# Seven half-size second products for two chunks of the first block, with their sums and the attention steps around them placed anew

## The chip, the cores and the metric

The kernel runs on one core of a Trainium2 chip. The core has five engines with queues of their own: TensorE (PE in the profile; its weight loads are listed apart as PEld), VectorE (DVE), ScalarE (ACT), GpSimd (POOL) and SyncE (SP), which issues most DMAs. Each engine takes its instructions in the order in which the program issues them and waits on semaphores for the others. The metric is the device time of one execution in microseconds (us).

## The reference

The program computes a linear attention with decay over 4 batches, 8 heads, 768 tokens and head size 64, and then a feed-forward layer with a squared relu:

```python
state = gamma * state + k[:, :, t] (outer) v[:, :, t]     # for each token t, per batch and head
y[:, :, t] = scale * q[:, :, t] @ state                   # scale = 1 / sqrt(64)
x = y, as 3072 tokens x 512
h = maximum(x @ w_in, 0)                                  # w_in  512 x 2048
out = (h * h) @ w_out                                     # w_out 2048 x 512
```

Inputs and output are float32 in HBM.

## The kernel before

**Tiling.** The 3072 tokens are 24 chunks of 128 (six for each batch). The feed-forward layer takes them in 11 blocks (`BLOCKS`, line 19): four chunks in block 0 and two in each other block. The hidden size 2048 is 16 groups f of 128; four groups are a quarter g. Matmuls read bf16 and accumulate in float32 in PSUM, in banks that hold 512 float32 values per partition.

**A block's feed-forward** (`ffn_pieces`, line 976) is a generator that yields after each piece of TensorE work. The first product (line 826) makes x @ w_in for a group f; ScalarE takes the relu out of PSUM into an `h` tile (line 835), and the squares are taken a little later by VectorE (line 806) or ScalarE. The second product multiplies the squares with w_out:

- In blocks 0 and 1 it is plain (`second`, line 1019): 16 matmuls of 512 columns for a chunk, one per f, into one bank. In block 0 all four chunks go together, quarter by quarter: g outside, chunks inside, so four banks are open. `store` (line 1030) has ScalarE copy each bank to `osb` and SyncE issue the output's DMA.
- From block 2 on (`SEVEN`) the two chunks are handled by `seven_products` (line 840). It is Strassen's scheme in Winograd's form: the two chunks, the two halves of the 2048 hidden values (even and odd f) and the two halves of the 512 outputs make a 2 x 2 by 2 x 2 product of blocks, done with seven half-size products of eight 256-wide matmuls each, where the plain way has eight. VectorE makes sums of the h blocks (`s1` to `s4`) and adds the products (`u`, `v`, `oa`, `ob`). The sums of w_out's blocks (`t1` to `t4`, tiles `w_sum`) are made once by `sum_w_out` (line 313): half 0 is made from w_out's quarters 0 and 1, half 1 from quarters 2 and 3. The seventh product of a block is kept (`kept`) and run among the first products of the next block.

**The loads of w_out.** Four DMAs on GpSimd's queue (`load_w_out`, line 169) bring a quarter each and convert it to bf16. They are issued at places 6, 8, 11 and 14.

**The order** is written out by hand. All engines' queues follow the program's order. `n` counts pieces: block 0's first four come before the loop, its first products for f = 4 to 15 are pieces 5 to 16, its second products pieces 17 to 32, and block 1 begins with piece 33. After piece n, `before(n)` (line 1204) issues what `put(n, ...)` has registered: the attention steps of later chunks, loads, casts and sums of w_out; and then the squares that are due. I say "place n" for that. `attend(m, scaled, places)` registers the steps of one chunk m: `scale_q` and `transpose_q` (for an even m, for both chunks of a pair: VectorE; then TensorE and a ScalarE copy), `scale_kv` (k on VectorE, v on GpSimd), `transpose_k` (TensorE, two ScalarE copies to `k_bd`), `scores` in two halves (TensorE, then VectorE's mask), `state` (TensorE, then ScalarE copies one half of the rows and VectorE the other) and `outputs` (TensorE, a ScalarE copy to `xt`).

**Buffers that matter here.** The pool `ps_f` (tiles `psf`) has four banks; `tp`, `st`, `y` and `c_ps` have one each, and transposes of q and of k share `tp`. `hpool` has three tiles of 4096 columns: `spare` (line 1052), which holds masked scores at the start, and the two h tiles of block 0; later blocks take one each in turn. `opool` has four output tiles. The tile framework makes an engine wait before it touches a PSUM bank of a tile that another engine still uses.

Of the kernel before, what the change touches and what calls it, by code (L numbers as in the profile page):

```python
# [9 lines left out]
FP32 = mybir.dt.float32  # L10
# [3 lines left out]
AF = mybir.ActivationFunctionType  # L14
ALU = mybir.AluOpType
# [16 lines left out]
def kernel(  # L32
# [9 lines left out]
    nc = tc.nc  # L42
    P = nc.NUM_PARTITIONS

    B, H, S, D = q.shape
    DM, DFF = moe_w_in.shape
    C = 128
    NCH = S // C
    NPAIR = H // 2
    NFB = DFF // 128  # L50
    NCB = DM // 128
    NQ = 4
    FPQ = NFB // NQ
# [22 lines left out]
    opool = ctx.enter_context(tc.tile_pool(name="opool", bufs=4))  # L76
    upool = ctx.enter_context(tc.tile_pool(name="upool", bufs=1))
# [4 lines left out]
    ps_f = ctx.enter_context(tc.tile_pool(name="ps_f", bufs=4, space=bass.MemoryType.PSUM))  # L82
# [105 lines left out]
    def exponents(pattern, step, name, logs, parts=(slice(0, P),)):  # L188
# [35 lines left out]
        out=ident[:],  # L224
# [11 lines left out]
        out=cmask[:],  # L236
# [10 lines left out]
    for rows in halves:  # L247
        nc.gpsimd.affine_select(
            out=maskp[rows],
# [58 lines left out]
    w_out_bf = [t[:, j * FPQ : (j + 1) * FPQ] for t in w_out_halves for j in range(2)]  # L308

    HN = DM // 2  # L310
    sums = [const.tile([P, NFB // 2, HN], BF16, name=f"w_sum{i}") for i in range(4)]

    def sum_w_out(half):

        src = w_out_halves[half].rearrange("s (j k) (n c) -> s k n j c", k=2, n=2)
        (b11, b12), (b21, b22) = ([src[:, k, n] for n in range(2)] for k in range(2))
        t1, t2, t3, t4 = (t[:, 4 * half : 4 * half + 4] for t in sums)
        for out, in0, in1 in ((t1, b12, b11), (t2, b22, t1), (t3, b22, b12), (t4, b21, t2)):
            yield nc.vector.tensor_tensor(out=out, in0=in0, in1=in1, op=ALU.subtract)
# [489 lines left out]
    h2s = {}  # L809

    def h_tiles(tb):
        wide = BLOCKS[tb] * C
        count = NFB * wide // 4096
        for _ in range(count):
            t = hpool.tile([P, 4096], BF16, name="h2")
            h2s.setdefault(tb, []).append(t.rearrange("e (f t) -> e f t", t=wide))

    def h_of(tb, f0, f1=None):
        n = NFB // len(h2s[tb])
        j, f = divmod(f0, n)  # L820
        return h2s[tb][j][:, f : f + (1 if f1 is None else f1 - f0)]

    def first_product(tb, hp, f, cols):
        g, fq = divmod(f, FPQ)
        for cb in range(NCB):
            nc.tensor.matmul(  # L826
                hp,
                lhsT=w_in_bf[g][:, cb, fq * 128 : (fq + 1) * 128],
                rhs=xts[tb][:, cb, cols],
                start=(cb == 0),  # L830
                stop=(cb == NCB - 1),
            )

    def relu(hv, hp, on_scalar=False):
        nc.scalar.activation(hv, hp[:], AF.Relu)  # L835
        squares.append((hv, on_scalar))

    kept = []

    def seven_products(tb):  # L840
# [115 lines left out]

        return first_sums, rest if tb + 1 < len(BLOCKS) else rest_at_end

    open_ps = {}

    def first_unit(tb, g, c, parts=(0, 1)):

        if tb not in h2s:
            h_tiles(tb)
        if (tb, g, c) not in open_ps:
            open_ps[tb, g, c] = ps_f.tile([P, FPQ, C], FP32, name="psf")
        hp = open_ps[tb, g, c]
        cols = slice(c * C, (c + 1) * C)
        half = FPQ // 2
        for part in parts:  # L970
            for fq in range(part * half, (part + 1) * half):
                first_product(tb, hp[:, fq, :], g * FPQ + fq, cols)
        if 1 in parts:
            relu(h_of(tb, g * FPQ, (g + 1) * FPQ)[:, :, cols], open_ps.pop((tb, g, c)))

    def ffn_pieces(tb):
        nch = BLOCKS[tb]
        TB = nch * C
        if tb == 0:
            for f in range(FPQ, NFB):  # L980
                hp = ps_f.tile([P, TB], FP32, name="psf")
                first_product(tb, hp[:], f, slice(0, TB))
                relu(h_of(tb, f)[:, 0], hp)
                yield
        elif tb <= 2:

            for c in range(nch):
                for g in range(NQ):
                    first_unit(tb, g, c)
                    if tb in SEVEN and (c, g) == (1, 3):  # L990
                        first_sums, rest = seven_products(tb)
                        first_sums(slice(0, 4))
                    yield
            if tb in SEVEN:
                yield from rest()
                return
        else:
            h_tiles(tb)
            per = 512 // TB
            if tb in SEVEN:  # L1000
                first_sums, rest = seven_products(tb)
            for f0 in range(0, NFB, per):
                hp = ps_f.tile([P, per, TB], FP32, name="psf")
                for f in range(f0, f0 + per):
                    first_product(tb, hp[:, f - f0, :], f, slice(0, TB))
                relu(h_of(tb, f0, f0 + per), hp, tb in SEVEN and f0 // per in (1, 3))
                if f0 // per in (1, 2, 3) and kept:
                    next(kept[0])
                if f0 // per == 4:
                    kept.clear()  # L1010
                if f0 // per == 5 and tb in SEVEN:
                    first_sums(slice(0, 4))
                yield
            if tb in SEVEN:
                yield from rest()
                return


        def second(op, j, g, cols=slice(0, DM)):
            for fq in range(FPQ):  # L1020
                f = g * FPQ + fq
                nc.tensor.matmul(  # L1022
                    op[:],
                    lhsT=h_of(tb, f)[:, 0, j * C : (j + 1) * C],
                    rhs=w_out_bf[g][:, fq, cols],
                    start=(f == 0),
                    stop=(f == NFB - 1),
                )

        def store(op, j, cols=slice(0, DM)):  # L1030
            osb = opool.tile([P, DM], FP32, name="osb")
            nc.scalar.activation(osb[:, cols], op[:], AF.Copy)
            r0 = (first[tb] + j) * C
            nc.sync.dma_start(out[r0 : r0 + C, cols], osb[:, cols])


        together = nch if tb == 0 else 1
        for j0 in range(0, nch, together):
            ops = [ps_f.tile([P, DM], FP32, name="psf") for _ in range(together)]
            for g in range(NQ):  # L1040
                for j, op in enumerate(ops):
                    second(op, j0 + j, g)
                    if g == NQ - 1:
                        store(op, j0 + j)
                    yield


    tp, st, f = (ps_tp, "tp"), (ps_st, "st"), (ps_f, "psf")
# [3 lines left out]
    spare = hpool.tile([P, 4096], BF16, name="h2")  # L1052
# [68 lines left out]
    start = [sum(npieces[:tb]) for tb in range(len(BLOCKS) + 1)]  # L1121
    parts = {}

    def put(place, what, *args):
        parts.setdefault(place, []).append((what, args))
# [4 lines left out]
    def attend(m, scaled, places):  # L1130
        if m % 2 == 0:
            put(scaled, scale_q, m, 0)
            put(scaled, scale_q, m, 1)
            put(places[0], transpose_q, m)
        put(places[0], scale_kv, m)
        put(places[1], transpose_k, m)
        put(places[2], scores, m, 0)
        put(places[3], scores, m, 1)
        put(places[3], state, m)
        put(places[4], outputs, m)  # L1140
# [20 lines left out]
    for m, which, place in ((6, "k", 16), (6, "v", 17), (7, "k", 18), (7, "v", 19)):  # L1161
        put(place, load_kv, m, which)
    put(10, cast_w, "in", 3)
    for half, at_places in enumerate(((25, 25, 25, 25), (31, 31, 48, 48))):
        made = sum_w_out(half)
        for place in at_places:
            put(place, next, made)
    attend(4, 21, (23, 25, 27, 29, 31))
    attend(5, None, (28, 30, 31, 32, 34))
    attend(6, 31, (33, 35, 37, 39, 42))  # L1170
    attend(7, None, (38, 42, 44, 46, 49))
    packed = pack_constants()
# [13 lines left out]
    for m, d in zip(range(PACK_FROM, NCHUNK), done):  # L1186
# [4 lines left out]
    places = {  # L1191
        (8, "k"): [22, 23, 24, 25, 33, 33, 34, 34],
        (8, "v"): [35 + j // 2 for j in range(8)],
        (12, "k"): [47, 48, 49, 50, 52, 53, 55, 56] + [74 + j for j in range(8)],
        (12, "v"): [58, 59, 60, 61, 62, 64, 65, 66] + [82 + j for j in range(8)],
        (18, "k"): [92 + 4 * j // 3 for j in range(8)] + [117 + 4 * j // 3 for j in range(8)],
        (18, "v"): [103 + 4 * j // 3 for j in range(8)] + [128 + 4 * j // 3 for j in range(8)],
    }
# [10 lines left out]
    n = BLOCKS[0]  # L1209
    before(n)  # L1210
    for tb in range(len(BLOCKS)):
        for _ in ffn_pieces(tb):
            n += 1
            before(n)
# [31 lines left out]
```

## Time and profile before

| what | us |
|---|---|
| median of 3 runs (lowest to highest) | 205.09 (204.23 to 205.53) |
| the profiled execution, as timed | 204.37 |
| its span, first to last instruction | 202.5 |
| TensorE busy | 195.7 |
| VectorE busy | 151.2 |
| ScalarE busy | 127.6 |
| GpSimd busy | 68.0 |

The granted TensorE clock is 1.000 over the whole span. The profile's page gives the busy time of each engine, the chain of work that ended last (each step led back to what released it) and the costliest groups of instructions by line. The trace answers finer questions: a timeline of one engine in a window, the busy time in a stretch, the time from a DMA's issue to its landing. A matmul's listed length holds the time until its result has left the array; matmuls overlap, so the cost of one in a stream is the step from one start to the next. In a group's row the figures after the bar are busy time, mean length in ns, and idle time before it with what ended it.

### The profile page before, as it was taken

What the parts mean: (1) busy time and instruction counts of PE and PEld (TensorE: products, weight loads), DVE (VectorE), ACT (ScalarE), POOL (GpSimd) and SP (SyncE); (2) the same over time, 40 slices, a digit from 0 to 9 for tenths busy, and PEclk for the clock granted to TensorE, in tenths of its full rate; (3) what the DMA queues carried; (4) which work ended last, traced back from release to release, by engine and by line L of the source; (5) the groups of instructions that cost most, each with busy time, mean ns of one, the idle gap of its engine ahead of it and who ended that gap; (6) DMA issues with size and microseconds to landing.
All of it is one profiled execution on the core that took longest, in us unless ns stands there. A gap on an engine that the chain in (4) does not pass through costs nothing.

```text
span 202.5 us, 5744 instructions
## 1 busy us (share of the span) xinstructions
PE 195.7 (97%) x2321; PEld 160.1 (79%) x2327; DVE 151.2 (75%) x309; ACT 127.6 (63%) x258; POOL 68.0 (34%) x131
## 2 busy tenths in 40 slices
PE   5899999999999999999999999999999999999993
PEld 1478444558965998988989999999889899999883
DVE  3986768268597888788798798798797797485374
ACT  8764872348853766782784785783775776763730
POOL 8693711311330552282225225252225225100000
PEclk9999999999999999999999999999999999999999
DMA  5999999999979478979979998979998254300202
GB/s 169 356 375 398 338 195 197 260 233 320 236 160 262 125 159 156 202 204 223 171 214 164 214 208 203 226 182 227 212 157 200 107 105 49 111 3 0 107 0 104
DMA packets 92250, 38.12 MB, mean 188 GB/s; under 512 B 68544, under 2 KB 88256, under 8 KB 92224
## 3 DMA queue, kind: packets, MB, share of 16 engines
q1 hardware_dynamic: 90112, 35.66, 72.3%
q0 software_dynamic: 2112, 2.10, 6.2%
q8 instruction: 18, 0.29, 0.6%
q14 instruction: 8, 0.07, 0.1%
HBM read 27.26 MB, written 6.29 MB: 166 GB/s over the span
## 4 chain that ended last, share of the span: by engine, by line
PE 89%; DVE 4%; DMA 2%; ACT 2%; issue 1%; DVEq 0%
PE psf L826 40%; PE psf L860 18%; PE psf L1022 10%; PE tp L860 7%; DMA qn<-in_q_dram 2%; PE y L783 2%; PE st L727 2%; PE y L776 2%; PE c_ps L754 2%; DVE h L806 1%; PE c_ps L627 1%; PE st L430 1%; PE y L506 1%; ACT h L835 1%; PE y L342 1%
## 5 line engine op out<-in xcount | busy, mean ns | idle before, releaser
L826 PE MATMUL psf<-xt,w_in_bf 128*128 128x256 bf16 (+2 forms) x879 | 92.2, 259 | 0.2 <-issue 0.2
L826 PEld LDWEIGHTS <-w_in_bf 128*128 128x128 bf16 x880 | 71.2, 98 | 11.4
L835 ACT ACTIVATE h<-psf 128x512 bf16<-128x512 f32 x96 | 56.1, 594 | 20.1 <-PE psf L826 18.5
L806 DVE TENSOR_TENSOR h<-h 128x512 bf16<-128x512 bf16 x80 | 35.6, 460 | 19.2 <-ACT h L835 18.8
L688 POOL CAST ks_bdp<-stage 64x512 bf16<-64x512 f32 x32 | 24.5, 767 | 38.7 <-issue 30.7
L705 POOL COPY v_bd<-v 64x512 bf16<-64x512 bf16 x32 | 20.6, 643 | 42.0 <-DVE v L697 36.7
L860 PEld LDWEIGHTS <-h 128*128 128x128 bf16 x288 | 26.3, 98 | 3.8 <-DVE h L806 1.0
L1022 PE MATMUL psf<-w_out_bf,h 128*128 128x512 bf16 x91 | 21.9, 379 | 0.4 <-issue 0.2
L860 PE MATMUL tp<-w_out_bf,h 128*128 128x256 bf16 x136 | 19.4, 273 | 0.2 <-DVE h L806 0.2
L860 PE MATMUL psf<-w_sum,h 128*128 128x256 bf16 x136 | 19.1, 273 | 0.0
L860 PE MATMUL psf<-w_sum,k_bd 128*128 128x256 bf16 x144 | 17.9, 273 | 0.0
L361 DVE TENSOR_TENSOR qs<-qn,qf 128x512 bf16<-128x512 f32 x20 | 16.3, 824 | 0.0
L1022 PEld LDWEIGHTS <-h 128*128 128x128 bf16 x96 | 8.9, 98 | 9.0
L860 PEld LDWEIGHTS <-k_bd 128*128 128x128 bf16 x144 | 13.7, 98 | 1.5
L763 ACT ACTIVATE s_bd<-c_ps 64x256 bf16<-64x256 f32 x29 | 10.7, 370 | 6.5 <-PE c_ps L754 6.5
L856 DVE TENSOR_TENSOR osb<-psf,u 128x256 f32<-128x256 f32 x26 | 10.3, 421 | 6.1 <-PE psf L860 5.8
L856 DVE TENSOR_TENSOR u<-psf,u 128x256 f32<-128x256 f32 x18 | 7.6, 423 | 8.9 <-PE psf L860 8.7
L697 DVE TENSOR_TENSOR v<-stage,kf 128x512 bf16<-128x512 f32 x16 | 12.5, 783 | 0.0
L764 ACT ACTIVATE s_bd<-c_ps 64x256 bf16<-64x256 f32 x29 | 11.0, 378 | 0.4
L734 DVE TENSOR_TENSOR pt<-st,cmask 128x512 bf16<-128x512 f32 x16 | 11.0, 687 | 0.1
L856 DVE TENSOR_TENSOR k_bd<-h 128x512 bf16<-128x512 bf16 x18 | 10.7, 597 | 0.3
L896 ACT ACTIVATE osb<-tp 128x256 f32<-128x256 f32 x8 | 3.1, 384 | 12.2 <-PE tp L860 12.2
(133 smaller groups left out, 262.4 us busy)
## 6 DMA issues: line engine op xcount, KB each, us to landing
qn<-in_q_dram SPq DMA_DIRECT2D x12, 512.0 KB, 4.9
out_dram<-osb SPq DMA_DIRECT2D x23, 256.0 KB, 2.4
stage<-in_k_dram SPq DMA_DIRECT2D x32, 96.0 KB, 3.4
stage<-in_v_dram SPq DMA_DIRECT2D x32, 96.0 KB, 3.5
stage<-in_moe_w_in_dram SPq DMA_DIRECT2D x4, 512.0 KB, 7.1
stage<-in_moe_w_in_dram SPq DMA_DIRECT2D x2, 1024.0 KB, 10.2
w_out_bf<-in_moe_w_out_dram POOLq DMA_DIRECT2D x4, 512.0 KB, 10.3
kn<-in_k_dram SPq DMA_DIRECT2D x6, 256.0 KB, 6.0
```

The costliest lines, as they stand in the source:

```text
L361: engine.tensor_tensor(out=out, in0=by, in1=table[:, :, None].to_broadcast([P, H, D]), op=ALU.mult)
L688: nc.gpsimd.tensor_copy(ks[rows, :, hh, :].rearrange("s (u p) d -> s u p d", u=2), kn[rows])
L697: nc.vector.tensor_tensor(out=v2.rearrange("s (u p) d -> s u p d", u=2), in0=vn, in1=kf2[:, i, :, :, None].to_broadcast([P, 2, NPAIR, D]), ...
L705: nc.gpsimd.tensor_copy(v_bd[rows, :, hh, :], v2[rows])
L734: nc.vector.tensor_tensor(out=pt[:], in0=st[:], in1=cmask2.rearrange("s r t -> s (r t)")[:, None, :].to_broadcast([P, 2 * NPAIR, C // 2]), ...
L764: nc.scalar.activation(s_bd[halves[1], :, 1, :], c[halves[1]], AF.Copy)
L806: nc.vector.tensor_mul(hv, hv, hv)
L826: nc.tensor.matmul(hp, lhsT=w_in_bf[g][:, cb, fq * 128 : (fq + 1) * 128], rhs=xts[tb][:, cb, cols], start=(cb == 0), stop=(cb == NCB - 1),)
L835: nc.scalar.activation(hv, hp[:], AF.Relu)
L856: nc.vector.tensor_tensor(out=out, in0=in0, in1=in1, op=op)
L860: nc.tensor.matmul(to, lhsT=left[:, j], rhs=right(j) if callable(right) else right[:, j], start=(start and j == 0), stop=(stop and j == NF ...
L1022: nc.tensor.matmul(op[:], lhsT=h_of(tb, f)[:, 0, j * C : (j + 1) * C], rhs=w_out_bf[g][:, fq, cols], start=(f == 0), stop=(f == NFB - 1),)
```

## The change

Chunks 0 and 1 of block 0 keep their plain second products. Chunks 2 and 3 get seven half-size products by a new function, `last_of_first`. Its sums s1, s2 and s4 lie in `spare`, and s3 takes the place of a21 in block 0's h tiles. The products share two psf banks: pa and pe lie in the halves of one, pd and pb in the halves of the other, and the first matmul of pa and that of pd clear their whole bank. The pieces of block 0 are now:

- 17 to 22: `plain(j)` for j = 0 to 5: the two chunks' 512-wide matmuls for f = 2j and 2j + 1, and one 256-wide matmul of a11 x b11;
- 23: the first halves of s1 x t1 and s2 x t2; 24: the first half of a22 x t4;
- 25 and 26: `plain(6)` and `plain(7)`, then ScalarE's copies of pa and of the two chunks, and their stores;
- 27: a12 x b21 on top of pa; 28 to 30: the second halves of the products with t1, t2 and t4; 31 and 32: s3 x t3, then VectorE's additions;
- 34, in block 1: the seventh product, s4 x b22; the two chunks' stores at 35 and 36.

The sums of h stand at places 11, 17 and 22. The sums of w_out's first half move from place 25 to 20; those of its second half from 31 and 48 to 23 and 27. Most steps of chunks 4 and 5 move up: chunk 4's `scale_q` from 21 to 13 and 15, `transpose_q` from 23 to 21, `scale_kv` from 23 to 18, the rest by two or three places; chunk 5's `scale_kv`, `transpose_k` and first scores by one to three.

```diff
@@ after seven_products
+    def last_of_first():
+        def halves_of(k, c):
+            return [
+                t.rearrange("e (j k) (c t) -> e k c j t", k=2, c=4)[:, k, 2 + c] for t in h2s[0]
+            ]
+        (a11, a12), (a21, a22) = ([halves_of(k, c) for k in range(2)] for c in range(2))
+        n = NFB // 4
...
+        s3 = a21
+        b = lambda k, c: lambda j: w_out_bf[j // 2][:, 2 * (j % 2) + k, c * HN : (c + 1) * HN]
...
+        def first_sums(x):
+            add(s1[x], a21[x], a22[x])
+            add(s2[x], s1[x], a11[x], ALU.subtract)
+        def last_sums():
+            for x in range(2):
+                add(s3[x], a11[x], a21[x], ALU.subtract)
+            for x in range(2):
+                add(s4[x], a12[x], s2[x], ALU.subtract)
+        def second_products():
+            ops = [ps_f.tile([P, DM], FP32, name="psf") for _ in range(2)]
+            pa, pe, pd, pb = (
+                t[:, n * HN : (n + 1) * HN]
+                for t in [ps_f.tile([P, DM], FP32, name="psf") for _ in range(2)]
+                for n in range(2)
+            )
...
+            for j in range(6):
+                plain(j)
+                yield
+            product(pd, s1, t1, lo)
+            product(pb, s2, t2, lo, False)
+            yield
+            product(pe, a22, t4, lo, False)
+            yield
+            plain(6)
+            yield
+            plain(7)
+            nc.scalar.activation(a[:], pa, AF.Copy)
+            for c, op in enumerate(ops):
+                osb = opool.tile([P, DM], FP32, name="osb")
+                nc.scalar.activation(osb[:], op[:], AF.Copy)
+                nc.sync.dma_start(out[c * C : (c + 1) * C], osb[:])
+            yield
+            product(pa, a12, b(1, 0), lo, False)
+            product(pa, a12, b(1, 0), hi, False)
+            nc.scalar.activation(oa[:, 0:HN], pa, AF.Copy)
+            yield
+            product(pd, s1, t1, hi)
+            yield
+            product(pb, s2, t2, hi)
+            add(u[:], pb, a[:])
+            yield
+            product(pe, a22, t4, hi)
+            yield
+            product(pb, s3, t3, lo, False)
+            yield
+            product(pb, s3, t3, hi, False)
+            add(v[:], pb, a[:])
+            add(ob[:, HN:DM], pd, v[:])
+            add(ob[:, 0:HN], pe, v[:])
+            def last_product():
+                product(pd, s4, b(1, 1), range(8), False)
+                add(oa[:, HN:DM], pd, u[:])
+                yield
+                nc.sync.dma_start(out[r0 + C : r0 + 2 * C], ob[:])
+                yield
+                nc.sync.dma_start(out[r0 : r0 + C], oa[:])
+                yield
+            kept.append(last_product())
+            yield
@@ ffn_pieces, block 0
+            first_sums, last_sums, second_products = last_of_first()
+            put(11, first_sums, 0)
+            put(17, first_sums, 1)
+            put(22, last_sums)
...
+            yield from second_products()
+            return
@@ ffn_pieces, blocks 1 and 2
+                    if c * NQ + g in (1, 2, 3) and kept:
+                        next(kept[0])
+                    if c * NQ + g == 4:
+                        kept.clear()
@@ attend
-            put(scaled, scale_q, m, 1)
+            put(scaled + 2 if m == 4 else scaled, scale_q, m, 1)
-        put(places[0], scale_kv, m)
+        put(18 if m == 4 else places[0], scale_kv, m)
@@ the places
-    for half, at_places in enumerate(((25, 25, 25, 25), (31, 31, 48, 48))):
+    for half, at_places in enumerate(((20, 20, 20, 20), (23, 23, 27, 27))):
-    attend(4, 21, (23, 25, 27, 29, 31))
-    attend(5, None, (28, 30, 31, 32, 34))
+    attend(4, 13, (21, 22, 24, 26, 29))
+    attend(5, None, (25, 28, 30, 32, 34))
```

More of the change, by code (lines that the diff above doesn't have):

```diff
@@ L957, in seven_products, with add, product, plain @@
         return first_sums, rest if tb + 1 < len(BLOCKS) else rest_at_end
+    def last_of_first():
[5 more added lines that the diff above has]
+        n = NFB // 4
+        s1, s2, s4 = (
+            [
+                t.rearrange("e (x j t) -> e x j t", x=2, t=C)[:, x]
+                for x in range(2)
+            ]
+            for t in (spare[:, i * HN * 4 : (i + 1) * HN * 4] for i in range(3))
+        )
+        s3 = a21
+        b = lambda k, c: lambda j: w_out_bf[j // 2][:, 2 * (j % 2) + k, c * HN : (c + 1) * HN]
+        t1, t2, t3, t4 = (lambda j, t=t: t[:, j] for t in sums)
+        def add(out, in0, in1, op=ALU.add):
+            nc.vector.tensor_tensor(out=out, in0=in0, in1=in1, op=op)
+        def product(to, left, right, js, start=True, stop=True):
+            for j in js:
+                nc.tensor.matmul(
+                    to,
+                    lhsT=left[j // n][:, j % n],
+                    rhs=right(j),
+                    start=(start and j == 0),
+                    stop=(stop and j == NFB // 2 - 1),
+                    skip_group_check=True,
+                )
+        def first_sums(x):
[12 more added lines that the diff above has]
+                for n in range(2)
+            )
+            oa, ob = (opool.tile([P, DM], FP32, name="osb") for _ in range(2))
+            a, u, v = (upool.tile([P, HN], FP32, name=f"u{i}") for i in range(3))
+            r0 = 2 * C
+            def plain(j):
+                for f in (2 * j, 2 * j + 1):
+                    for c, op in enumerate(ops):
+                        nc.tensor.matmul(
+                            op[:],
+                            lhsT=h_of(0, f)[:, 0, c * C : (c + 1) * C],
+                            rhs=w_out_bf[f // FPQ][:, f % FPQ, :],
+                            start=(f == 0),
+                            stop=(f == NFB - 1),
+                        )
+                product(pa, a11, b(0, 0), (j,))
+            lo, hi = range(0, 4), range(4, 8)
+            for j in range(6):
[10 more added lines that the diff above has]
+            nc.scalar.activation(a[:], pa, AF.Copy)
+            for c, op in enumerate(ops):
+                osb = opool.tile([P, DM], FP32, name="osb")
[29 more added lines that the diff above has]
+            yield
+        return first_sums, last_sums, second_products
@@ L1034, in store @@
             nc.sync.dma_start(out[r0 : r0 + C, cols], osb[:, cols])
-        together = nch if tb == 0 else 1
-        for j0 in range(0, nch, together):
-            ops = [ps_f.tile([P, DM], FP32, name="psf") for _ in range(together)]
+        for j in range(nch):
+            op = ps_f.tile([P, DM], FP32, name="psf")
             for g in range(NQ):
[L1041 to L1045, printed above, removed]
+                second(op, j, g)
+                if g == NQ - 1:
+                    store(op, j)
+                yield
     tp, st, f = (ps_tp, "tp"), (ps_st, "st"), (ps_f, "psf")
```

## The prediction

> **What bounds the kernel now.** I read the page's busy shares first, then the chain that ended last.
>
> ```profile
> PE 195.7 (97%) x2321; PEld 160.1 (79%) x2327; DVE 151.2 (75%) x309; ACT 127.6 (63%) x258; POOL 68.0 (34%) x131
> ...
> PE 89%; DVE 4%; DMA 2%; ACT 2%; issue 1%; DVEq 0%
> ```
>
> TensorE is busy 97% of the span and is 89% of the chain. Removing a matmul therefore shortens the run by its step, provided that no new wait appears. The window table finds it busy 16.54 of 16.70 us in the changed stretch, 30.9 to 47.6. So next I read TensorE's timeline there (columns: start, length, engine, line, operation, tiles, count):
>
> ```profile
> 30.92 6.21 PE L1022 MATMUL psf<-w_out_bf,h 128*128 128x512 bf16 x27
> 36.96 0.61 PE L391 MATMUL tp<-ident,qs 128*128 128x128 bf16 x8
> 37.41 1.89 PE L1022 MATMUL psf<-w_out_bf,h 128*128 128x512 bf16 x8
> 39.13 0.39 PE L404 MATMUL tp<-ident,ks 128*128 128x128 bf16 x4
> ...
> 44.57 1.03 PE L1022 MATMUL psf<-w_out_bf,h 128*128 128x512 bf16 x4
> ...
> 47.63 1.06 PE L826 MATMUL psf<-xt,w_in_bf 128*128 128x128 bf16 x16
> ```
>
> The second products begin at 30.92, and block 1 at 47.63. From 37.41 to 39.13 stand eight 512-wide matmuls: one steps 1.72 / 8 = 0.215 us. The chain in order of time gives the half-wide step, 0.87 / 8 = 0.109 us:
>
> ```profile
> 37.57 1.73 PE psf L1022 x8
> 77.49 0.87 PE psf L860 x8
> ```
>
> The first use of w_out's quarter 2 is piece 25. Its place follows eight pieces of 0.86, from 30.92, and the transposes at 36.96 to 37.41, at about 38.3. The loads show when it could have been used:
>
> ```profile
> 21.96 1.73 POOL L170 DMA_DIRECT2D w_out_bf<-in_moe_w_out_dram  x2
> 24.66 1.48 POOL L170 DMA_DIRECT2D w_out_bf<-in_moe_w_out_dram  x2
> DMA to landing us min/median/max: 11.1/11.1/11.1
> DMA to landing us min/median/max: 7.1/10.3/13.8
> ```
>
> The third line is the issue at 24.66 alone; the fourth is all four. The first (21.96) takes 7.1 and the last (25.39) 13.8. Quarters 0 to 3 thus land at 29.0, 32.4, 35.8 and 39.1; for the second, issued at 22.9, the pair's figures 7.1 and 9.5 give 32.4. Before, quarters 2 and 3 are needed about 2.5 and 5 us after they land, so no wait is visible.
>
> **What goes.** Chunks 2 and 3 cost 32 x 0.215 = 6.9 us as 512-wide matmuls. Seven half products are 56 x 0.109 = 6.1. TensorE loses eight steps: **-0.87 us**. Within block 0 the saving is 1.7, because the seventh product (0.87) runs in piece 34. The stretch before held 0.22 us of small waits (46.10 to 46.35 and at 47.4), which I count as gone: **-0.22**.
>
> **What becomes late: quarter 2.** Pieces 17 to 22 now take both chunks' matmuls for two f, plus one half-wide matmul: 4 x 0.215 + 0.109 = 0.97 us. Piece 21 (f = 8, first of quarter 2) starts at 30.92 + 4 x 0.97 = 34.8. The quarter lands at 35.8 and TensorE takes its matmuls in order: **+1.0**. The loads' places, and everything issued ahead of them, are unchanged, so I leave the landing alone. Quarter 1 is needed at 32.9 and lands at 32.4. Quarter 3 is needed only at piece 25, about 40.4: the three half products at 23 and 24 do cover that wait.
>
> **The attention steps moved up.** transpose_q 4 now stands at 21 and transpose_k 4 at 22; both use the one "tp" buffer. ScalarE's copy out of it (L397) takes 1.02 us and began 0.2 after the last transpose was issued. One piece (0.97) lies between, where before there were two: **+0.3**. Scores of chunk 4 (place 24) follow transpose_k by 1.3 us in place of 1.7, against 0.2 + 1.21 for its two copies (L411): **+0.1**. In piece 27, a12 x b21 continues the bank that ScalarE must first copy to `a` (0.38, row L884). Between lie only four scores and four state matmuls, 0.45: **+0.2**.
>
> **The queue behind the last sums.** On VectorE, first_sums(0) and chunk 4's q scaling (about 2.2 us: 0.6 + 0.46 per first_sums pair by rows L856, single ones 0.42 to 0.83, 2 x 0.6 by L361) go into the 3.2 us that it idled among the squares. After the last square (32.2) come first_sums(1) 1.0, ks 0.6, four w_sum 3.0 and last_sums 1.4, ending near 38. The next sums wait for quarter 3 (39.1) and end at 40.5. Queued behind them is the mask of chunk 4's first scores, done at 41.3; TensorE needs its buffer at 42.3. So that wait is covered by 1.0 us. Then this chain, seen before:
>
> ```profile
> 43.73 0.36 ACT L481 ACTIVATE s_bd<-c_ps 64x256 bf16<-64x256 f32 x1
> 44.18 0.43 DVE L483 CAST s_bd<-c_ps 64x256 bf16<-64x256 f32 x1
> 44.64 0.69 DVE L319 TENSOR_TENSOR w_sum<-w_out_bf 128x1024 bf16<-128x1024 bf16 x1
> 45.37 0.69 DVE L319 TENSOR_TENSOR w_sum<-w_out_bf,w_sum 128x1024 bf16<-128x1024 bf16 x1
> ```
>
> VectorE's state copy begins 0.09 after ScalarE's, though the two read different rows. In the new order ScalarE first does `a` (42.5), then two 0.5 evictions, then its state copy, to 44.2. VectorE's copy follows to 44.6, then t3 and t4 of the second half (now place 27) to about 45.9. Piece 30 needs that t4. TensorE gets there at 42.9 + 0.87 (27) + 0.44 (28) + 0.22 (transposes) + 0.44 (29) + 0.67 (outputs 4) = 45.55: **+0.4**. The small waits of scores 5 and transpose_q 6 behind VectorE's u, mask and two q scalings are **+0.15**.
>
> The Trainium skill, "PSUM — Partial Sum Buffer" (PSUM bank collisions), has collisions per bank and quadrant of partitions, and lets different quadrants be accessed at once. By that the two state copies need not be serial, t4 would be ready near 44.7 and the 0.4 would vanish. The row at 44.18 shows them serial here, so I keep 0.4.
>
> **At no cost.** VectorE's u, v, ob and oa (0.42 each, rows L856), and ScalarE's `a` and `oa` (0.38 each in place of two 0.6 evictions), end before the bank they read is written again: u by 46.2, piece 31 at 46.6; ob from pd by 49.5, the seventh product near 50.1. Without that cover each would cost its lateness, at most 0.5. Two products in a bank tie pe's second half (piece 30) to ScalarE's read of pa for `oa`, over by 44.5, before TensorE comes at 45.6. Block 1's h tile takes one of hpool's three buffers; if it were `spare`'s, its first relu would wait for the seventh product (51), with four psf banks to run on: 0 to 0.5, and I take 0, since both of block 0's h tiles are free by then. VectorE then trails block 1's squares by about 2 us, which products at piece 41, eight pieces on, don't need sooner. The moved casts on POOL still wait for v of chunk 4 (34.9), as before. On SyncE the stores of chunks 2 and 3 go behind four stage loads; SyncE was issuing out at 47.2 to 49.3, long after their data, and both new stores are ready (50.0, 51.6) as it reaches them. Moving t3 and t4 from place 48 frees 1.4 us of VectorE at 64.6, where TensorE showed no wait on it.
>
> **Sum.** -0.87 - 0.22 + 1.0 + 0.3 + 0.1 + 0.2 + 0.4 + 0.15 = **+1.1 us**. TensorE is full afterwards, so it carries to the end. The profiled execution took 204.37 (span 202.5 and 1.9 around it): 205.4. The median of the runs is 0.72 higher, 205.09, so I predict **206.1**. Bounds: the waits other than quarter 2's lie between 0 (the neighbours run early) and twice their 1.15; quarter 2's between 0 and 2.
>
> **Rivals.** *The quarter is in time*: the wait in piece 21 vanishes if the quarter lands 1 us sooner. Against: three landings 3.3 to 3.4 us apart, a steady stream. 205.4 - 1.0 = 204.4, as a median 205.1: chance 0.21. *The saving comes through*: the t4 queue and tp waits are hidden too, since ScalarE and VectorE idled here (6.48 and 10.28 busy of 16.70): 205.09 - 0.6 = 204.5: chance 0.15.
>
> *Slower by over 1%*: the w_out stream itself. Before, 2.5 us of slack hid its jitter; now piece 21 follows it one for one. A stream 7% slower over the 13.8 us from first issue to quarter 2's landing adds 1.0. It also uses the 1.0 of cover of the mask behind quarter 3; any slip past that adds again. 207.1 or more; it decides from 0.9 of slip. For it: the third and last transfers took 11.1 and 13.8 from issue while SyncE's loads ran too. Against: the runs spread over 1.3 us only. Chance 0.16.
>
> *Half-wide products don't save*: weight loads set the pace. Rows: a load is 98 ns, a half-wide step 109 ns with its load hidden. If the load were exposed, 56 x 0.098 = 5.5 us would be lost: 210.6. Chance 0.02. The Trainium skill, "TensorE: Matmul & The Clock Gate" (Back-to-back issue gap), states a sustained 131 ns per 512-wide matmul among its loads and 81 ns at 128. By that, 32 x 0.131 = 4.2 us would become between 56 x 0.081 = 4.5 and 7.3 (an estimate), a loss. This trace's 215 and 109 ns contradict it.
>
> **Chances.** Forecast 0.46, the others as given. About 1% (2.05 us) is what a measurement of this kernel can tell from no change. Faster by more would need 2 us where the removed work is 0.87: 0.02. Slower by more is about half of the stream's case, the pace case and the forecast's tail: 0.13. Within: 0.85. The range goes from the saving case less half the runs' spread (204.0) to the stream's case (207.3).
>
> **What would show it.** In the changed kernel's TensorE timeline: a gap near 34.8 ended by w_out's transfer; one before chunk 4's k transposes ended by ScalarE L397; one before the half products with t4's second half ended by VectorE's w_sum; eight half-wide matmuls inside block 1. With no gap at 34.8 I am wrong by 1 us; with w_sum done before piece 30, by 0.4. A later squares or h wait in block 1 would be a cost that I have at nothing.

## The result, and the profile after

The changed kernel takes 205.36 us (median of 22 runs, 205.17 to 206.47), the kernel before 204.83 in the same comparison (22 runs, 204.22 to 205.69). The ratio is 1.003, with a 95% interval of 1.0016 to 1.0044: slower by about half a microsecond. The forecast was slower by 1.0 to 1.1, at 206.1. The profiled executions differ by 0.9: 205.27 against 204.37, with spans of 203.4 and 202.5.

These are the page's busy shares and chain for the changed kernel, to be held against those of before:

```profile
PE 195.3 (96%) x2346; PEld 162.2 (80%) x2351; DVE 155.2 (76%) x322; ACT 127.2 (63%) x258; POOL 66.4 (33%) x131
...
PE 73%; DMA 11%; SPq 6%; DVE 4%; ACT 3%; issue 1%; POOL 0%; DVEq 0%
```

TensorE's busy time fell by only 0.4, as the listed lengths overlap. The chain shows more: it was TensorE for 89% and now runs through DMA for 11% and SyncE's queue for 6%, because from some point back it follows a transfer. TensorE's timeline of the stretch names the transfer (columns as before; line 1017 is the 512-wide product, line 984 the half-wide ones):

```profile
34.71 0.27 PE L984 MATMUL psf<-w_out_bf,h 128*128 128x256 bf16 x1
35.86 1.02 PE L1017 MATMUL psf<-w_out_bf,h 128*128 128x512 bf16 x4 [0.88 <-DMA w_out_bf<-in_moe_w_out_dram]
...
38.14 0.27 PE L984 MATMUL psf<-w_out_bf,h 128*128 128x256 bf16 x1
38.55 0.38 PE L404 MATMUL tp<-ident,ks 128*128 128x128 bf16 x4
...
42.58 0.39 PE L458 MATMUL c_ps<-v_bd,ks 128*128 128x128 bf16 x4
42.99 1.03 PE L984 MATMUL psf<-w_out_bf,h 128*128 128x256 bf16 x8
...
45.52 0.28 PE L506 MATMUL y<-pt,v_bd 128*128 128x128 bf16 x2
45.99 0.61 PE L984 MATMUL psf<-w_sum,h 128*128 128x256 bf16 x4 [0.20 <-DVE w_sum L319]
...
47.83 1.06 PE L826 MATMUL psf<-xt,w_in_bf 128*128 128x128 bf16 x16
...
50.06 1.04 PE L984 MATMUL psf<-w_out_bf,h 128*128 128x256 bf16 x8
...
51.60 1.06 PE L826 MATMUL psf<-xt,w_in_bf 128*128 128x128 bf16 x16
```

A wait is read from the steps: the last start before it, plus that matmul's step, against the next start. At 34.71 + 0.11 = 34.82 TensorE is ready for plain(4), and begins at 35.86: 1.04 us for quarter 2. At 38.25 it is ready for chunk 4's k transposes and begins at 38.55: 0.30 for ScalarE's copy out of `tp`. At 42.80 against 42.99: 0.19 for the copy of pa. At 45.63 against 45.99: 0.36 for t4. The seventh product stands at 50.06, and piece 35 begins at 51.60, where before it began at 50.54: **+1.06**. At the end +0.9 is left, since a wait of 0.19 on VectorE's squares at 75.9 in the profile before is 0.03 here.

So the profiled execution came out as the sum had it. What has to be explained is why the runs as a whole lost only half as much.

### The profile page after: what moved, and what is told of

Read it like the earlier page. It is cut to its first block, busy times and chain, and to the rows that moved or that the text cites. A ratio compares the mean times of both kernels' runs of the same rounds, so it can differ in the third digit from the quotient of the medians.

```text
span 203.4 us, 5804 instructions
## 1 busy us (share of the span) xinstructions
PE 195.3 (96%) x2346; PEld 162.2 (80%) x2351; DVE 155.2 (76%) x322; ACT 127.2 (63%) x258; POOL 66.4 (33%) x131
## 4 chain that ended last, share of the span: by engine, by line
PE 73%; DMA 11%; SPq 6%; DVE 4%; ACT 3%; issue 1%; POOL 0%; DVEq 0%
PE psf L826 32%; PE psf L860 18%; PE tp L860 7%; DMA w_out_bf<-in_moe_w_out_dram 6%; DMA stage<-in_moe_w_in_dram 5%; PE psf L1149 3%; SPq L164 3%; SPq L115 2%; PE psf L984 2%; PE y L783 2%; PE st L727 2%; PE y L776 2%; PE c_ps L754 2%; PE psf L1017 1%; DVE h L806 1%
## 5 line engine op out<-in xcount | busy, mean ns | idle before, releaser
L688 POOL CAST ks_bdp<-stage 64x512 bf16<-64x512 f32 x32 | 23.0, 718 | 37.6 <-issue 23.3
L860 PEld LDWEIGHTS <-h 128*128 128x128 bf16 x288 | 26.3, 98 | 3.6 <-DVE h L806 0.7
L790 ACT ACTIVATE xt<-y 128x512 bf16<-128x512 f32 x16 | 9.6, 598 | 1.8 <-PE y L783 1.2
L804 ACT ACTIVATE h<-h 128x512 bf16<-128x512 bf16 x16 | 10.1, 630 | 0.5
```

The source lines that it names most:

```text
L688: nc.gpsimd.tensor_copy(ks[rows, :, hh, :].rearrange("s (u p) d -> s u p d", u=2), kn[rows])
L860: nc.tensor.matmul(to, lhsT=left[:, j], rhs=right(j) if callable(right) else right[:, j], start=(start and j == 0), stop=(stop and j == NF ...
```

## Experiments

Theory: the terms were right, and the executions of the kernel before lie between two times some 0.9 us apart, because of something early that delays TensorE but not the w_out stream; the new wait for quarter 2 takes that delay up. Rivals: something later gives the saving or loss back; or few of the changed kernel's executions were late by chance. The runs of the kernel before make the theory possible. In one comparison of 29, twelve have a span of 202.5, ten of 203.5 or more, and seven lie between; of the 22 of the changed kernel, fourteen lie at 203.3 to 203.5.

### The kernel before, profiled again

> The kernel before, unchanged, for one more profile. If its execution falls in the upper cluster of times (205.2 to 205.5), the first theory expects the 0.9 us to have come before the second products start (30.9 in the first profile, then 31.8), with w_out's four quarters landing where they did, at 29.0, 32.4, 35.8 and 39.1, and the stretch from there to the end as long as before. The rival expects the same start and a later stretch longer. In the lower cluster it should repeat the first profile to 0.1 us.

This execution took 205.36, with a span of 203.6. TensorE's early timeline, first in this execution, then in the first profile of the same kernel:

```profile
6.42 0.63 PE L342 MATMUL y<-ident 128*128 128x512 bf16 x1
6.85 0.63 PE L584 MATMUL psf<-ident,ks_bdp 128*128 128x128 bf16 x4
7.28 1.02 PE L342 MATMUL y<-ident 128*128 128x512 bf16 x2
8.13 0.39 PE L550 MATMUL psf<-ident,qs 128*128 128x128 bf16 x4
...
31.94 6.21 PE L1022 MATMUL psf<-w_out_bf,h 128*128 128x512 bf16 x27
```

```profile
6.46 0.38 PE L342 MATMUL y<-ident 128*128 128x512 bf16 x1
6.69 0.40 PE L584 MATMUL psf<-ident,ks_bdp 128*128 128x128 bf16 x4
6.92 0.59 PE L342 MATMUL y<-ident 128*128 128x512 bf16 x2
```

From one start to the next the same idle matmul takes 0.43 in the late execution and 0.23 in the first. TensorE keeps the slow pace until 8.1 us there, and until 6.4 in the first. I call this a late clock. It is read from these steps alone: the profile's own column for the granted clock shows 1.00 over this stretch in both executions. The second products then begin at 31.94 in place of 30.92: 1.02 later, and from there to the end it is 171.7 against 171.6.

The slow pace is only a part of the 1.02. It makes VectorE's first mask 0.64 late (8.97 against 8.33). Behind the mask VectorE scales a part of k, which TensorE then transposes (the late execution's line first):

```profile
9.58 1.04 DVE L559 TENSOR_TENSOR ks_bdp<-kn,kfp 128x512 bf16<-128x512 f32 x1
9.04 0.69 DVE L559 TENSOR_TENSOR ks_bdp<-kn,kfp 128x512 bf16<-128x512 f32 x1
```

GpSimd scales another part of k at that time. In the first execution VectorE begins just ahead of it, at 9.04, and GpSimd's, begun at 9.09, takes 1.55. In the late one GpSimd begins ahead, at 9.03, and takes 1.04, and VectorE's takes 0.35 longer. The transposes start at 10.68 in place of 9.79. A third profile, that of both orders below (a kernel with the same start), has the fast pace already at 7.3 and the mask at 8.70, yet VectorE's scaling takes 1.36 there, the transposes start at 10.72 and the second products at 31.95. In these profiles a delay of 0.4 and one of 0.6 thus end as the same 0.9, which fits two times better than an even spread. No run changed this order of the two engines, and the seven executions between the two times stay unexplained.

The w_out loads in the late execution:

```profile
24.84 1.48 POOL L170 DMA_DIRECT2D w_out_bf<-in_moe_w_out_dram  x2
DMA to landing us min/median/max: 10.9/10.9/10.9
```

The second line is the issue at 24.84 alone: quarter 2 lands at 35.7, where it landed at 35.8. TensorE is 1 us late and the stream is not. The Trainium skill, "TensorE: Matmul & The Clock Gate" (the HAM clock gate), says that the full clock follows a stretch of about 3.4 us of activity by a window that runs freely, so that it comes at another moment in each execution. The two profiles agree: 6.4 and 8.1 us with the same program.

### The late clock, made to happen

```diff
-    keep_awake(7, pool=ps_y, name="y")
+    keep_awake(2, pool=ps_y, name="y")
```

The edit was made in both kernels. In the kernel before:

> The kernel before with 2 in place of 7 of the matmuls on idle data at the very start (line 1053), so that TensorE's full clock should be granted later in every execution, as it was by chance at 8.1 in place of 6.4 us in the second profile of the kernel before. They write nothing that is used. First theory: TensorE reaches the second products later by some d (about 1 us or more) and the w_out quarters land as ever; this kernel has no wait for them, so its time rises by d: 205.3 or more at the lower end. Rival (the second cluster isn't due to the clock's start): the time stays at 204.2 to 204.5 at the lower end.

In the changed kernel:

> The changed kernel with the same edit. First theory: its wait for quarter 2 takes up the first 1.0 us of the delay d that the edit gives the kernel before, so the profile shows the gap before plain(4) smaller by d (gone from d = 1.04 on), and its time rises by d - 1.04 or not at all; at d = 1.0 to 1.2 it is then level with the kernel before under the same edit or faster by up to 0.2, at 205.2 to 205.4. Rival: the w_out stream starts later with TensorE, the gap stays near 1.0 and the time rises by d as well: 206.2 or more.

The kernel before took 205.65 (205.23 to 205.98, 12 runs); none of them came near 204.4. In its profile the fast pace begins at 9.1, the second products at 31.92 and block 1 at 48.64, 1.0 later than in the first profile. (With the pace this late VectorE's scaling of k starts only at 10.01 and takes its usual 0.68; the transposes start at 10.76, about as late as in the late execution above.) The changed kernel took 205.55 (205.21 to 205.76, 12 runs), 0.2 above its time without the edit, though its second products begin at 32.19, 1.26 later than in its own first profile (the fast pace begins at about 10.8). This is its timeline at piece 21:

```profile
32.19 0.81 PE L1017 MATMUL psf<-w_out_bf,h 128*128 128x512 bf16 x3
...
35.97 0.27 PE L984 MATMUL psf<-w_out_bf,h 128*128 128x256 bf16 x1
36.15 1.02 PE L1017 MATMUL psf<-w_out_bf,h 128*128 128x512 bf16 x4
```

TensorE is ready at 36.08 and begins at 36.15, just as quarter 2 lands (36.1): the wait of 1.04 has become 0.07. With a late clock both kernels cost the same; with an early one the changed kernel is 0.9 slower, by the two first profiles. That is the theory, shown with the late clock set by hand.

### Quarter 2 not awaited

This version leaves the wait out: two of the eight steps read quarter 0 in place of quarter 2.

```diff
-                            rhs=w_out_bf[f // FPQ][:, f % FPQ, :],
+                            rhs=w_out_bf[(0, 1, 0, 3)[f // FPQ]][:, f % FPQ, :],
...
-                product(pa, a11, b(0, 0), (j,))
+                product(pa, a11, lambda j: b(0, 0)(j - 4 if j in (4, 5) else j), (j,))
```

> The changed kernel, but plain(4) and plain(5) and their two matmuls of a11 x b11 read quarter 0 of w_out in place of quarter 2, so that TensorE doesn't wait for quarter 2 in piece 21 (this computes another output: those parts use the wrong quarter). First theory: the sum was right term by term, the 1.0 us wait is really paid by an execution like the profiled one, and the times of the kernel before lie in two clusters some 0.9 us apart because of something early that delays TensorE but not the w_out stream; the wait swallows that delay in the changed kernel. Then the profile shows no gap near 34.8, block 1's first unit at about 46.8 in place of 47.83, a profiled execution near 204.3 (or 205.2 if it falls in the upper cluster), and times that spread over 0.9 us as those of the kernel before do. Rival: what is saved here is given back later, since another transfer or VectorE is late next: 205.0 to 205.3, with a new gap before piece 26 or in block 1. Second rival: the two clusters come from somewhere else, and the changed kernel had few of the upper ones by chance: 204.3 with the same narrow spread as the changed kernel.

It took 204.48 (204.21 to 205.26, 12 runs), 0.9981 of the kernel before (0.9961 to 1.0001). The gap is gone and block 1 begins at 46.79, 1.04 before the changed kernel's 47.83. The lower end, 204.21, is 0.96 below the changed kernel's, and the times spread over 1.0 again. The profiled execution (204.56) shows 0.34 given back at 58.9, where `outputs` waits for VectorE's mask: a square at 54.0 that takes 0.43 in the changed kernel's profile took 0.83, and VectorE's queue stayed 0.4 late up to the mask. So the second rival (narrow spread) is out, and the first holds for a third of a microsecond in the profiled execution.

### w_out issued earlier

```diff
-    for g, place in enumerate((6, 8, 11, 14)):
+    for g, place in enumerate((6, 8, 8, 8)):
```

> The changed kernel with w_out's loads issued at places 6, 8, 8 and 8 in place of 6, 8, 11 and 14, so that quarters 2 and 3 are issued about 0.9 us earlier, ahead of GpSimd's last casts of w_in. First theory: the quarters land 3.3 to 3.4 us apart because the stream itself is that slow, so quarter 2 still lands at 35.6 to 35.9 and the gap before plain(4) stays (1.0, less what a late clock start takes). Rival: the issue sets the landing, quarter 2 lands at 34.9 and the gap falls by 0.9.

Quarter 2 was issued at 23.7 in place of 24.6 and landed at 35.7; the wait is 0.92. Behind an unmoved quarter 1 the landing follows the stream, not the issue, so an earlier place for quarters 2 and 3 alone doesn't remove the wait. Issuing the whole stream earlier, quarters 0 and 1 too, was not tried. The one execution took 205.47, with the mask's wait of the last experiment again (0.32 at 59.8).

### Half products ahead of quarter 2

```diff
-            for j in range(6):
+            for j in range(4):
                 plain(j)
                 yield
             product(pd, s1, t1, lo)
             product(pb, s2, t2, lo, False)
             yield
+            for j in (4, 5):
+                plain(j)
+                yield
...
-    attend(4, 13, (21, 22, 24, 26, 29))
+    attend(4, 13, (20, 22, 24, 26, 29))
```

> The changed kernel with piece 23 (first halves of s1 x t1 and s2 x t2) moved ahead of plain(4), and chunk 4's transposes of q at place 20 in place of 21: 0.45 + 0.87 us of TensorE work that needs no quarter 2 stand where it is awaited. First theory: the gap of 1.04 before plain(4) and the 0.30 before chunk 4's k transposes vanish; quarter 3 (lands at 39.2) is now awaited for 0.2 to 0.3 before plain(6), and the mask behind the sums of quarter 3 for 0.2 before chunk 4's second scores; the `a` wait (0.19) is covered by that. Sum -0.7 to -0.9: 204.4 to 204.6 for an execution like the profiled one, so level with the kernel before. Rival (the saving is given back behind quarter 3): 205.0 to 205.3, with a gap of 1 us before plain(6).

It took 204.18 (203.98 to 205.14, 12 runs), 0.9974 of the kernel before (0.9953 to 0.9996): faster, where at best level was expected. Its timeline:

```profile
34.82 0.61 PE L391 MATMUL tp<-ident,qs 128*128 128x128 bf16 x8
35.26 1.04 PE L984 MATMUL psf<-w_sum,h 128*128 128x256 bf16 x8
36.14 1.03 PE L1017 MATMUL psf<-w_out_bf,h 128*128 128x512 bf16 x4
...
39.14 1.02 PE L1017 MATMUL psf<-w_out_bf,h 128*128 128x512 bf16 x3
...
44.71 0.61 PE L984 MATMUL psf<-w_sum,h 128*128 128x256 bf16 x4 [0.20 <-DVE w_sum L319]
```

The transposes and eight half-wide matmuls fill 34.82 to 36.14, and quarter 2 has landed by then (35.7). The `tp` wait went too. Quarter 3 costs 0.2 before 39.14, and the mask 0.2 before chunk 4's second scores; block 1 begins at 46.55, 1.28 earlier than in the changed kernel, where 0.7 to 0.9 was expected. I had set these two waits 0.1 too high together, and left the waits of the scores (0.10) and of the copy of pa (0.19), which went as well, out of the sum. The last line shows t4's wait unchanged.

### The last sums of w_out earlier

```diff
-    for half, at_places in enumerate(((20, 20, 20, 20), (23, 23, 27, 27))):
+    for half, at_places in enumerate(((20, 20, 20, 20), (23, 23, 25, 25))):
```

> The changed kernel with t3 and t4 of w_out's second half at place 25 in place of 27, so that they don't stand behind VectorE's copy of chunk 4's state, which waits for ScalarE. First theory: the 0.37 gap before piece 30 vanishes, t4 is done near 42.6 and nothing else is late: -0.3 to -0.4, a profiled execution of 204.9. Rival: VectorE is too full, the mask of chunk 4's second scores or chunk 5's k scaling comes late instead, and the time stays within 0.1 of the changed kernel.

It took 205.04 (204.87 to 205.52, 12 runs), 0.32 below the changed kernel and 1.0014 of the kernel before (0.9996 to 1.0032), so level with it. VectorE's timeline shows t4 (the first line) done at 42.6, ahead of its state copy and not behind it:

```profile
41.91 0.68 DVE L319 TENSOR_TENSOR w_sum<-w_out_bf,w_sum 128x1024 bf16<-128x1024 bf16 x1
...
43.12 0.68 DVE L437 TENSOR_TENSOR pt<-st,cmask 128x512 bf16<-128x512 f32 x1
44.30 0.43 DVE L483 CAST s_bd<-c_ps 64x256 bf16<-64x256 f32 x1 [0.49 <-ACT s_bd L481]
```

The mask is late by 0.3 and nobody waits for it. The wait before piece 30 is gone; the copy's own wait for ScalarE, which the prediction put in this chain, is still there and now costs nothing.

### Both orders

> Both orders of the last two experiments at once: half products and chunk 4's q transposes ahead of plain(4), and t3 and t4 of w_out's second half at place 25. First theory: the two savings stand at different waits and add up: 0.37 less than with the half products moved alone (profiled 203.99), so 203.6 at the lower end and a median of 203.8, faster than the kernel before by 0.4 to 0.6%. Rival: with TensorE 1 us earlier VectorE is late next (mask of chunk 4's second scores, k scaling of chunk 5) and less than 0.15 of the 0.37 remains: 203.85 at the lower end, median 204.1.

> Both orders at once, unchanged, for a profile with TensorE's clock granted early (the last one had it at 7.3 us and the second products at 31.95). Then all waits but three are expected gone: about 0.25 for quarter 3 before plain(6), 0.2 for the mask before chunk 4's second scores, and 0.07; the gap of 0.37 before piece 30 is gone, and 0.15 of it comes back at one of the former, which would explain that the lower end was 203.76 and not 203.6. With the clock late again, it repeats the last profile.

With both edits: 204.46 (203.76 to 204.83, 12 runs) against 205.35 of the kernel before beside it, a ratio of 0.9961 (0.9943 to 0.9979). It is faster than the kernel before. The median expected was 203.8, and this is 0.7 above it and above the 204.18 of the half products moved alone. How often the clock is late differs between comparisons: beside this one, 14 of the kernel before's 29 executions had a span of 203.5 or more, in the earlier one 10 of 29, and its median was 205.35 in place of 204.84. So I compare profiled executions of like clock: with an early one 202.0 against 202.5, with a late one 202.7 against 203.6. These are single executions.

The profile of the twelve had a late clock (second products at 31.95) and no wait for w_out at all. The second one (203.86) had an early clock:

```profile
39.15 1.02 PE L1017 MATMUL psf<-w_out_bf,h 128*128 128x512 bf16 x3
...
41.28 0.38 PE L430 MATMUL st<-qT,k_bd 128*128 128x128 bf16 x4
...
44.42 0.60 PE L984 MATMUL psf<-w_sum,h 128*128 128x256 bf16 x4
...
46.25 0.94 PE L826 MATMUL psf<-xt,w_in_bf 128*128 128x128 bf16 x14
```

Block 1 begins at 46.25, 0.30 before the version with the half products moved alone, so there the savings add up nearly in full (0.05 goes to chunk 5's k scaling). The lower end fell by 0.22 only: 0.17 is given back at 58.3, where `outputs` waits for the mask, as in two experiments above.

## Why the prediction was right, and where it was wrong

**The terms.** Against the profile of the changed kernel: quarter 2 +1.0 (1.04), `tp` +0.3 (0.30), scores behind `k_bd` +0.1 (0.10), the copy of pa +0.2 (0.19), t4 +0.4 (0.36), scores 5 and transpose_q 6 +0.15 (0.07, the latter none), eight steps less -0.87 (the seventh product's eight take 0.87 at 50.06), old waits gone -0.22. Sum +1.1; measured +1.06 at piece 35 (the single waits, read from rounded starts, add to 0.98) and +0.9 at the end. The sum's time for the profiled execution, 205.4, was 205.27. One landing was added up 0.1 too low: quarter 3's is 25.39 + 13.8 = 39.2, and nothing hung on it.

**The step that failed** is the last one: "The median of the runs is 0.72 higher, 205.09, so I predict 206.1." I carried the gap between profile and median over to the changed kernel as if it were noise that rides on any kernel. It is a delay before 22 us that follows a late clock; the 0.72 came from three runs, and over 22 it was 0.46. A change that adds a wait on a transfer which doesn't share the delay absorbs it: the changed kernel's median is 0.09 above its profiled execution. So the likely cost was not 1.1 for every execution but 0.9 to 1.1 for those with an early clock and about 0 for those with a late one. The runs show 0.5 to 0.6 on the whole.

**What I had in hand.** The forecast noted that "piece 21 follows it one for one", for a stream that is late. The other half, that TensorE being late is free at piece 21, was not drawn. The range (204.0 to 207.3) holds the time, and no change by over 1% came.

**The rivals.** The quarter in time is out: it landed between 35.7 and 36.1 in every profile, later with the clock edit (36.1) and not earlier with the issue moved. The stream slipping by 1 us was not seen in any profile. Four of the changed kernel's 22 executions are 0.8 to 1.2 above the others (206.08 to 206.47); no profile shows one of these, so whether the stream was late in them stays open. (The latest landings in a profile are 0.3 late for quarter 2 and 0.8 for quarter 3, both with the clock edit.) The saving coming through was out for the change as placed, and is what the last version gets. Weight loads don't set the pace: half-wide matmuls step 0.109 in every stretch here.

**Costs put at nothing.** u, v, ob and oa came in time. "A later squares or h wait in block 1 would be a cost that I have at nothing": the changed kernel's own profile has none, but three of the experiments lose 0.17 to 0.34 near 58 to 60 us at a mask, behind one slow operation of VectorE: a square in two of them, a scaling of q (0.85 in place of 0.62) in both orders. The queue is 0.24 to 0.41 late in these, and all but 0.07 of it comes through as a wait, so the cover there is under 0.1.

**The rule on banks** of the Trainium skill ("PSUM — Partial Sum Buffer", PSUM bank collisions), by which the two state copies need not be serial, did not set the order here. ScalarE's copy ended at 44.17 and VectorE's began at 44.20 in the changed kernel, with ScalarE's named as what it waited for. The copy did wait, and the 0.36 before piece 30 is what that cost. That fits the tile framework's guard of a whole bank; no run shows what the chip alone would allow.

## What to carry to other kernels

When work is cut ahead of a transfer, place the first use of each piece of the transfer against its landing, quarter by quarter, and put work that doesn't need it in front of it: the same seven products, in another order and with two sums earlier, go from 0.3% slower to 0.4% faster, each against the kernel before beside it. Before a profile's difference is put on a median, find out what spreads the runs; a delay early in the kernel is swallowed by any later wait that doesn't share it, so a slower order can look better than its profile, and taking that wait out again brings the spread back. Where an engine's queue holds work that waits for a late arrival, look at what stands behind it: two places' move of two sums was worth 0.3 us.

## What the runs showed that I had not expected

- TensorE's fast pace began at 5.1 to 8.1 us in the profiles of kernels with the same start, and at 9.1 and 10.8 with five idle matmuls fewer. Where it began at 8.1, the kernel before took 1.0 us more, half a per cent, all of it before 22 us.
- The w_out stream hardly moved with what stands around it: quarter 2 landed at 35.7 with its load issued 0.9 us earlier, at 35.7 with TensorE 1 us late, and at 36.1 at the latest.
- One VectorE square of a usual 0.43 us took 0.83 and 0.81 in two experiments, which was enough to make TensorE wait 0.3. In both, a GpSimd cast had begun 0.06 and 0.08 before it (at 53.95 and 54.83, 0.6 long), and the square ended 0.27 and 0.28 after the cast. In the changed kernel's own profile the square began 0.05 ahead of the cast and took 0.43; the cast then took 0.85. It looks like the scaling of k at 9 us: whichever of the two engines begins second is held up. No run separated the two, so this is not shown.
